# An attention and top-k kernel on one core: where the query split, the selection's flags and the one-hot steps stand in the lists of POOL and DVE

## The chip, the cores and the metric

One of the eight cores of a Trainium2 chip runs the whole program. The metric is the device time of one execution in microseconds, and lower is better. The kernel before took 926.11 us (median of three runs, 923.66 to 931.63). The engines are named as the profile names them: PE multiplies matrices (PEld is its weight load), DVE is the vector engine, ACT the scalar engine, POOL is GpSimd, SP issues most of the DMAs.

## The reference

```python
# attention; q is (4, 12288, 128), kv is (4, 384, 32, 128)
kv_pool = kv.reshape(B, H // 4, 4, W // 4, 4, C).mean(axis=(2, 4))
k = v = kv_pool.reshape(B, -1, C) @ w_sr          # 768 keys a batch
s = (q @ k.transpose(0, 2, 1)) / np.sqrt(C)
a = np.exp(s - s.max(-1, keepdims=True))
x = (a / (a.sum(-1, keepdims=True) + 1e-09)) @ v
# routed MLP: per batch, the 128 tokens with the largest score
scores = np.einsum('bsd,d->bs', x, w_gate)
top_idx = np.argpartition(-scores[b], capacity)[:capacity]
h = np.maximum(x[b, top_idx] @ w1, 0.0)
g = 1.0 / (1.0 + np.exp(-scores[b, top_idx]))
out[b, top_idx] = x[b, top_idx] + g[:, None] * (h @ w2)
```

## The kernel before

The queries are cut into blocks of 256 rows, 48 blocks a batch and 192 in all. The main loop makes one pass over `i` for each block. In pass `i` DVE takes the row maxima of block `i` (`s_max`, the tile `m`), PE makes the scores of block `i + 1` (`S`), ACT makes the exponentials of block `i` (`exp`, the tile `am`), and PE multiplies the probabilities of block `i - 4` by the values (`AV`, into the PSUM tile `o_two`; `LAG` is 4). The probabilities go through `hl`: ACT writes the high halves (`to_high`), POOL the low halves of 1280 columns (`to_low(i, 0, pool)`), DVE those of 256 columns, and two DMA transposes, issued by SP, bring them to `at`. After that DVE normalizes block `i - 4`: `sums`, `recip` (which adds two halves of `o_two` into its columns 260 to 388) and `finish`, the last reader of `o_two`, which writes `x`. The order on each engine is the order in which the program is written: `InOrder` ties each instruction to the one before it on its engine.

Three kinds of further work are generators, which the loop moves on by one step at named places (`at_point`, lines 765 to 812). A generator says with `yield "d"` that its next step belongs at the place "d", which is the last of a pass.

- `next_keys(b + 1)` (line 344) runs during batch `b`, so in the first three batches. For each of six key tiles it has six steps at "d", in which POOL adds up the 16 taps: four quarter sums, one sum over the whole tile, and two last sums, which write `pooled`. One pass after the "d" that follows, at "pe", `key_tile` (line 406) multiplies `pooled` by the weights on PE (two matmuls in the trace's names `s<-pooled,w_k` and `s<-w_in,pooled`). "pe" lies on PE between the high and the low half of `AV`. For the keys of batch 1 the generator starts at once, so that `pooled` is written in passes 5, 11, 17, 23, 29 and 35, all odd, and multiplied two passes later. For batches 2 and 3 it first lets five passes go by, and `pooled` falls in even passes.
- `topk(b)` (line 558) selects the 128 largest scores of batch `b` during the following batch (the last batch is done after the loop in another way). It turns the scores into an integer `key`, finds the threshold of the upper 16 bits in 16 steps of one pass each, makes flags (`gth`, `eqh`, `rest`), finds the threshold of the lower bits in 16 more steps, and makes `mask`. Key, flags and masks stand at "d", each once a batch.
- `pick(b, mask)` (line 604) turns the masks into indices by one-hot matrices (`ge`, then `oh`), gathers the rows, runs the MLP on them and writes them back.

`split_q` (line 422) cuts a pair of query blocks into a high part (`qh`, ACT) and a low part (`ql`, POOL), for `S`. In even passes `i` it is called on line 771 for blocks `i + 2` and `i + 3`, ahead of the pass's `to_low(i, 0, pool)` and behind the "d" of pass `i - 1`. The first use of `ql` is the second matmul of `S(i + 2)`, in pass `i + 1`.

Of the kernel before, what the change touches and what calls it, by code (L numbers as in the profile page):

```python
# [9 lines left out]
BF16 = mybir.dt.bfloat16  # L10
I32 = mybir.dt.int32
U32 = mybir.dt.uint32
U16 = mybir.dt.uint16
AF = mybir.ActivationFunctionType
ALU = mybir.AluOpType
# [4 lines left out]
P = 128  # L20
# [12 lines left out]
VC = C + 2  # L33
# [37 lines left out]
def attention_topk_mlp(ctx, tc, a, outs, capacity):  # L71
# [350 lines left out]
    def split_q(b, blk):  # L422
        ch, h = divmod(blk, BPC)
        raw = qraw[b, ch][:, h * BLK:(h + 2) * BLK]
        qh = qs.tile([P, 2 * BLK], F32R, name="qh")
        ql = qs.tile([P, 2 * BLK], BF16, name="ql")
        act.copy(qh, raw)
        pool.tensor_tensor(out=ql, in0=raw, in1=qh.bitcast(F32), op=ALU.subtract)
        for i in range(2):
            h, l = (x[:, i * BLK:(i + 1) * BLK] for x in (qh, ql))  # L430
            qsplit[b, blk + i] = h, h.bitcast(BF16).rearrange("p (q s) -> p q s", s=2)[:, :, 1], l
# [75 lines left out]
    def turn(n, h):  # L507
        k = cut(n) if by_pe(n) else 2 * M
        sp.dma_start_transpose(out=st[n]["at"][:, h, 0:k // P], in_=st[n]["hl"][:, h, 0:k])
# [26 lines left out]
    def recip(n):  # L536
        b, blk = blocks[n]
        dve.reciprocal(st[n]["rz"], st[n]["rz"])
        if st[n]["two"]:
            st[n]["o"] = o_two[:, :, 2 * VC:2 * VC + VL]  # L540
            dve.tensor_reduce(out=st[n]["o"], in_=o_two[:, :, 0:2 * VC].rearrange("p j (h c) -> p j c h", h=2)[:, :, 0:VL], axis=AX.X, op=ALU.add)
        if b not in scores:
            scores[b] = tk.tile([P, NCOL], F32, name="sc")
        dve.tensor_tensor(out=scores[b][:, blk * QT:(blk + 1) * QT], in0=st[n]["o"][:, :, C], in1=st[n]["rz"], op=ALU.mult)
# [13 lines left out]
    def topk(b):  # L558
        sc = scores.pop(b)
        th = tk.tile([P, 1], F32, name="th")  # L560
        pool.memset(th, float(1 << 15))
        tl = tk.tile([P, 1], F32, name="tl")
        pool.memset(tl, float(1 << 15))
        yield "d"
        key = tk.tile([P, NCOL], I32, name="key")
        dve.tensor_scalar(out=key, in0=sc.bitcast(I32), scalar1=31, scalar2=-(1 << 31), op0=ALU.arith_shift_right, op1=ALU.bitwise_or)
        dve.tensor_tensor(out=key, in0=key, in1=sc.bitcast(I32), op=ALU.bitwise_xor)
        halves = key.bitcast(U16).rearrange("p (n h) -> p n h", h=2)
        low, high = halves[:, :, 0], halves[:, :, 1]
        junk, eqh, rest, gth = (tk.tile([P, NCOL], t, name=x) for x, t in (("junk", BF16), ("eqh", U16), ("rest", U16), ("gth", BF16)))  # L570

        def search(x, t, need):
            for s in range(15, -1, -1):
                yield "cmp"
                cnt = tk.tile([P, 1], BF16, name="cnt")
                dve.tensor_scalar(out=junk, in0=x, scalar1=t, scalar2=None, op0=ALU.is_ge, op1=ALU.add, accum_out=cnt)
                yield "pe"
                pe.matmul(room["count"], ones16, cnt, start=True, stop=True)
                yield "up"
                up = tk.tile([P, 1], F32, name="up")  # L580
                dve.tensor_scalar(out=up, in0=room["count"], scalar1=need, scalar2=float(1 << s), op0=ALU.is_ge, op1=ALU.mult)
                yield "t"
                dve.tensor_scalar(out=t, in0=up, scalar1=-float(1 << (s - 1)) if s else -1.0, scalar2=t, op0=ALU.add, op1=ALU.add)

        yield from search(high, th, float(capacity))
        yield "d"
        above, need = tk.tile([P, 1], BF16, name="cnt"), tk.tile([P, 1], F32, name="need")
        dve.tensor_scalar(out=gth, in0=high, scalar1=th, scalar2=None, op0=ALU.is_gt, op1=ALU.add, accum_out=above)
        dve.tensor_scalar(out=eqh, in0=high, scalar1=th, scalar2=None, op0=ALU.is_equal)
        dve.tensor_tensor(out=rest, in0=low, in1=eqh, op=ALU.mult)  # L590
        yield "pe"
        pe.matmul(room["count"], ones16, above, start=True, stop=True)
        yield "up"
        dve.tensor_scalar(out=need, in0=room["count"], scalar1=-1.0, scalar2=float(capacity), op0=ALU.mult, op1=ALU.add)
        yield from search(rest, tl, need)
        yield "d"
        mask = tk.tile([P, 2, NCOL], BF16, name="mask")
        dve.scalar_tensor_tensor(out=mask[:, 0], in0=rest, scalar=tl, in1=gth, op0=ALU.is_gt, op1=ALU.add)
        dve.scalar_tensor_tensor(out=mask[:, 1], in0=rest, scalar=tl, in1=eqh, op0=ALU.is_equal, op1=ALU.mult)
        yield from pick(b, mask)  # L600
# [3 lines left out]
    def pick(b, mask):  # L604
# [20 lines left out]
        copy(ecol[0:NCOL], e_ps[0:NCOL])  # L625
        yield "d"
        dve.tensor_tensor(out=ecx[0:NCOL], in0=ecol[0:NCOL], in1=inc[0:NCOL, :, P - 1], op=ALU.subtract)
        yield "d"
        copy(pay[0:NCOL, :, 0], ecx[0:NCOL])
        for j0 in range(0, capacity, P):  # L630
            n = min(P, capacity - j0)
# [7 lines left out]
                dve.tensor_scalar(out=jr, in0=small, scalar1=float(j0), scalar2=None, op0=ALU.add)  # L639
            took = tk.tile([P, 2], F32, name="took")  # L640
            for s in range(2):
                dve.tensor_scalar(out=ge[0:NCOL, s], in0=jr[0:NCOL], scalar1=ecol[0:NCOL, s:s + 1], scalar2=None, op0=ALU.is_ge, op1=ALU.add, accum_out=took[0:NCOL, s:s + 1])
            yield "d"
            for s in range(2):
                dve.scalar_tensor_tensor(out=oh[0:NCOL, s], in0=jr[0:NCOL], scalar=ecx[0:NCOL, s:s + 1], in1=ge[0:NCOL, s], op0=ALU.is_ge, op1=ALU.subtract)
            yield "pe"
            g_ps = small_psum([P, P])
# [91 lines left out]
    def at_point(point):  # L739
        advance(vals, point)  # L740
        for tasks in (select, prep) if point == "pe" else (prep, select):
            advance(tasks, point)
# [4 lines left out]
    for i in range(nb):  # L747
        old = i >= LAG
        b, blk = blocks[i]
        if blk % 2 == 0 and i + AHEAD < nb and i + AHEAD >= BPC:  # L750
            nb_, nblk = blocks[i + AHEAD]
            load_q(nb_, nblk // BPC, nblk % BPC * BLK, (nblk % BPC + 2) * BLK)
        if blk == 0 and b + 1 < B:
            start(prep, next_keys(b + 1))
        if i == 0:
            sp.dma_start(out=w1, in_=a["w1"])
            sp.dma_start(out=w2, in_=a["w2"].rearrange("(t f) d -> f t d", f=P))
            ahead.append(load_kv(1, 2))
        if i:
            borrow(s_flat[(i - 1) % 2])  # L760
        s_max(i)
        if old:
            for j in range(QT):
                AV(i - LAG, j, halves=(0,))
            at_point("pe")
            for j in range(QT):
                AV(i - LAG, j, halves=(1,))
        else:
            at_point("pe")
        if i % 2 == 0 and i + 2 < nb:  # L770
            split_q(*blocks[i + 2])
        InOrder.seen.clear()
        at_point("ev")
        bank1 = list(InOrder.seen)
        InOrder.seen.clear()
        at_point("up")
        at_point("g")
        more = 0 < i < nb - 1
        bank0 = list(InOrder.seen)
        if more:  # L780
            if not old:
                warm(12, s_flat[(i + 1) % 2][:, 1024:1024 + P], bank0 + bank1)
            free = {3: bank0 + bank1, 2: bank0, 1: bank0, 0: ()}
            for part, term in ((3, LOW), (2, LOW), (3, HIGH), (2, HIGH)):
                S(i + 1, part, term, free[part])
        exp(i, 2 if by_pe(i) else 1)
        if by_pe(i):
            turn_pe(i)
        exp(i, 1 if by_pe(i) else 2)
        InOrder.seen.clear()  # L790
        at_point("a")
        for x in InOrder.seen:
            for y in st[i + 1]["far"]:
                tc.declare_no_dep(x, y, reason="other banks")
        if more:
            for part, term in ((1, HIGH), (0, HIGH), (1, LOW), (0, LOW)):
                S(i + 1, part, term, free[part])
        to_high(i, 1)
        if old:
            sums(i - LAG)  # L800
            recip(i - LAG)
            finish(i - LAG)
        at_point("t")
        at_point("cmp")
        at_point("v")
        to_low(i, 1, dve)
        exp(i, 0)
        to_high(i, 0)
        turn(i, 0)
        to_low(i, 0, pool)  # L810
        turn(i, 1)
        at_point("d")
        if old and blocks[i - LAG][1] == NBLK - 1:
            start(select, topk(blocks[i - LAG][0]))
# [272 lines left out]
```

## Time and profile before

| | us |
|---|---|
| median of three runs | 926.11 |
| lowest and highest | 923.66, 931.63 |
| the profiled execution | 927.06 |
| its span, first to last instruction | 925.3 |
| PE busy | 874.1 |
| DVE busy | 791.3 |
| POOL busy | 747.3 |
| ACT busy | 741.8 |

A pass is told in the trace by the start of DVE's reduction `m<-s`: there are 192, and the distance of two is the time of a pass. A line of the timeline gives start and duration in us, the engine, the operation, the tiles it writes and reads, and in brackets the engine's idle time before it with what ended it. Transfers and weight loads that lie close together are merged into one line with a count.

### The profile page before, as it was taken

The page shows a single profiled execution, that of the slowest core. Times are in us where ns is not written, and L with a number is a line of the kernel's source. Part 1 is how long each engine was busy: PE and PEld are TensorE (multiplying, and loading weights), DVE is VectorE, ACT ScalarE, POOL GpSimd, SP SyncE. Part 2 cuts the span into 40 slices and gives each one's busy share as a digit, 9 for nine tenths or more (in the row PEclk, how much of TensorE's full clock was granted, in tenths as well). Part 3 has the DMA queues.
Part 4 walks back from the last instruction along what each step waited for, and adds up shares of the span by engine and source line. Part 5 has one row for each costly group of instructions (what it writes and reads, how often), then busy time and mean ns, then how long its engine had stood idle before and what let it go on. Part 6 is the DMA issues. An engine that isn't in the chain of part 4 may idle for free.

```text
span 925.3 us, 21379 instructions
## 1 busy us (share of the span) xinstructions
PE 874.1 (94%) x7785; PEld 683.6 (74%) x7785; DVE 791.3 (86%) x1935; ACT 741.8 (80%) x1148; POOL 747.3 (81%) x486
## 2 busy tenths in 40 slices
PE   4899999999999999999999999999999999999966
PEld 3578778777777767777787777777787777777756
DVE  5888888888898888898889889898879999999943
ACT  2788888889878777888978888788898999888831
POOL 2699999989788888988888989888888877777732
PEclk9999999999999999999999999999999999999999
DMA  8999999999999999999999999999999999999990
GB/s 312 302 210 235 253 235 244 217 219 213 216 221 208 238 227 247 237 232 230 211 216 232 244 213 224 243 247 238 212 222 215 247 243 234 251 247 247 236 181 27
DMA packets 564124, 211.10 MB, mean 228 GB/s; under 512 B 532368, under 2 KB 533648, under 8 KB 563376
## 3 DMA queue, kind: packets, MB, share of 16 engines
q1 hardware_dynamic: 563696, 209.06, 109.4%
q8 instruction: 61, 1.00, 0.5%
q0 software_dynamic: 320, 0.66, 0.3%
q14 instruction: 47, 0.39, 0.1%
HBM read 52.04 MB, written 25.49 MB: 84 GB/s over the span
## 4 chain that ended last, share of the span: by engine, by line
PE 51%; DVE 16%; POOL 11%; DMA 9%; issue 7%; ACT 4%; DVEq 0%; POOLq 0%; SPq 0%; another core or an unknown queue 0%; ACTq 0%
PE s L56 28%; PE o_two L56 23%; DMA at<-hl 8%; DVE m L56 6%; POOL hl L56 5%; POOL kv_sum L56 3%; ACT am L56 2%; POOL ql L56 2%; DVE o_two L56 2%; DVE hl L56 1%; DVE rz L56 1%; DVE x L56 1%; DMA kv_raw<-in_kv 1%; ACT hl L56 1%; DVE kv_raw L56 1%
## 5 line engine op out<-in xcount | busy, mean ns | idle before, releaser
L56 POOL TENSOR_TENSOR hl<-am,hl 128x1280 bf16<-128x1280 f32 x192 | 504.1, 2626 | 125.0 <-ACT hl L56 88.9
L56 PEld LDWEIGHTS <-at 128*128 128x128 f16 (+1 forms) x4656 | 363.9, 97 | 95.3 <-DMA at<-hl 17.9
L56 PE MATMUL o_two<-vx,at 128*128 128x259 f16 (+1 forms) x4548 | 421.8, 246 | 11.8 <-DMA at<-hl 8.4
L56 ACT ACTIVATE am<-s,m 128x512 f32<-128x512 f32 (+1 forms) x528 | 357.9, 706 | 51.1 <-DVE m L56 36.2
L56 DVE TENSOR_REDUCE m<-s 128x2 f32<-128x1536 f32 x192 | 336.4, 1752 | 14.1 <-PE s L56 13.0
L56 ACT CAST hl<-am 128x1280 f16<-128x1280 f32 x192 | 241.6, 1258 | 6.0
L56 PE MATMUL s<-kb,ql 128*128 128x512 bf16 (+1 forms) x769 | 240.2, 326 | 3.2 <-POOL ql L56 3.2
L56 PE MATMUL s<-kl,qh 128*128 128x512 bf16 (+1 forms) x769 | 241.8, 328 | 0.4 <-ACT ecol L56 0.4
L56 PE MATMUL s<-kh,qh 128*128 128x512 f32 (+1 forms) x769 | 215.7, 376 | 1.2 <-ACT kh L56 0.7
L56 DVE TENSOR_REDUCE o_two<-o_two 128x258 f32<-128x516 f32 x188 | 128.4, 683 | 0.0
L56 POOL TENSOR_TENSOR ql<-q_raw,qh 128x512 bf16<-128x512 f32 x96 | 122.4, 1275 | 2.0 <-ACT qh L56 2.0
L56 PEld LDWEIGHTS s<-kh,qh 128*128 128x128 f32 x769 | 116.5, 190 | 6.2 <-ACT kh L56 0.9
L56 PEld LDWEIGHTS <-qh 128*128 128x128 bf16 x769 | 74.8, 97 | 52.9 <-issue 29.6
L56 ACT CAST at<-s 128x256 f16<-128x256 f32 x144 | 53.6, 372 | 67.1 <-PE s L56 67.1
L56 PEld LDWEIGHTS <-ql 128*128 128x128 bf16 x769 | 75.4, 98 | 33.7 <-POOL ql L56 7.9
L56 DVE TENSOR_SCALAR rz<-o_two,sg 128x2 f32<-128x2 f32 x189 | 41.2, 218 | 44.0 <-PE o_two L56 41.3
L56 DVE TENSOR_TENSOR x<-o_two,rz 128x256 f32<-128x256 f32 x189 | 78.4, 415 | 0.0
L56 DVE TENSOR_TENSOR at<-s,at 128x256 bf16<-128x256 f32 x144 | 60.8, 422 | 9.7 <-ACT at L56 4.7
L56 PE MATMUL s<-cst,am 128*128 128x128 f32 x288 | 56.1, 276 | 4.4 <-ACT am L56 4.0
L56 ACT CAST qh<-q_raw 128x512 fp32r<-128x512 f32 x96 | 58.8, 613 | 0.0
L56 POOL TENSOR_TENSOR kv_sum<-kv_raw 128x256 f32<-128x256 f32 x72 | 52.4, 728 | 0.0
L56 PEld LDWEIGHTS s<-cst,am 128*128 128x128 f32 x288 | 35.7, 139 | 16.8 <-ACT am L56 11.0
(163 smaller groups left out, 528.9 us busy)
## 6 DMA issues: line engine op xcount, KB each, us to landing
out<-x SPq DMA_DIRECT2D x96, 256.0 KB, 3.3
q_raw<-in_q SPq DMA_DIRECT2D x94, 256.0 KB, 3.3
kv_raw<-in_kv SPq DMA_DIRECT2D x37, 512.0 KB, 4.9
at<-hl SPq DMA_TRANSPOSE x384, 3.9
kv_raw<-in_kv SPq DMA_DIRECT2D x5, 1024.0 KB, 8.5
w<-in_w SPq DMA_DIRECT2D x2, 512.0 KB, 10.7
kv_raw<-in_kv SPq DMA_DIRECT2D x2, 256.0 KB, 4.8
q_raw<-in_q SPq DMA_DIRECT2D x1, 512.0 KB
```

The costliest lines, as they stand in the source:

```text
L56: r = f(*args, **kwargs)
```

## The change

`split_q` for blocks `i + 3` and `i + 4` is called at the end of odd passes `i`, behind `to_low(i, 0, pool)` and ahead of that pass's "d"; before, the same blocks were split at the start of the even pass behind it. (Pass 0 still splits blocks 2 and 3.) Key, flags and masks move from "d" to a new place "k", which lies between `recip` and `finish`; the place "t" (the threshold's update) moves ahead of `finish` as well. `gth` and `eqh` move from SBUF to columns of `o_two` in PSUM that the attention leaves free, and the first half of the key is written there too. The four one-hot instructions, which stood two and two at two "d" places, stand one each at "cmp", "d", "cmp" and "d" of the same two passes.

```diff
--- before.py
+++ after.py
@@ -562,12 +562,16 @@
         tl = tk.tile([P, 1], F32, name="tl")
         pool.memset(tl, float(1 << 15))
         yield "d"
+        yield "k"
+        side = [o_two[:, j, 2 * VC + VL:2 * VC + VL + NCOL] for j in range(2)]
+        flip = side[0].bitcast(I32)
         key = tk.tile([P, NCOL], I32, name="key")
-        dve.tensor_scalar(out=key, in0=sc.bitcast(I32), scalar1=31, scalar2=-(1 << 31), op0=ALU.arith_shift_right, op1=ALU.bitwise_or)
-        dve.tensor_tensor(out=key, in0=key, in1=sc.bitcast(I32), op=ALU.bitwise_xor)
+        dve.tensor_scalar(out=flip, in0=sc.bitcast(I32), scalar1=31, scalar2=-(1 << 31), op0=ALU.arith_shift_right, op1=ALU.bitwise_or)
+        dve.tensor_tensor(out=key, in0=flip, in1=sc.bitcast(I32), op=ALU.bitwise_xor)
         halves = key.bitcast(U16).rearrange("p (n h) -> p n h", h=2)
         low, high = halves[:, :, 0], halves[:, :, 1]
-        junk, eqh, rest, gth = (tk.tile([P, NCOL], t, name=x) for x, t in (("junk", BF16), ("eqh", U16), ("rest", U16), ("gth", BF16)))
+        junk, rest = (tk.tile([P, NCOL], t, name=x) for x, t in (("junk", BF16), ("rest", U16)))
+        gth, eqh = side
 
         def search(x, t, need):
             for s in range(15, -1, -1):
@@ -583,17 +587,17 @@
                 dve.tensor_scalar(out=t, in0=up, scalar1=-float(1 << (s - 1)) if s else -1.0, scalar2=t, op0=ALU.add, op1=ALU.add)
 
         yield from search(high, th, float(capacity))
-        yield "d"
+        yield "k"
         above, need = tk.tile([P, 1], BF16, name="cnt"), tk.tile([P, 1], F32, name="need")
         dve.tensor_scalar(out=gth, in0=high, scalar1=th, scalar2=None, op0=ALU.is_gt, op1=ALU.add, accum_out=above)
         dve.tensor_scalar(out=eqh, in0=high, scalar1=th, scalar2=None, op0=ALU.is_equal)
-        dve.tensor_tensor(out=rest, in0=low, in1=eqh, op=ALU.mult)
+        dve.tensor_tensor(out=rest, in0=eqh, in1=low, op=ALU.mult)
         yield "pe"
         pe.matmul(room["count"], ones16, above, start=True, stop=True)
         yield "up"
         dve.tensor_scalar(out=need, in0=room["count"], scalar1=-1.0, scalar2=float(capacity), op0=ALU.mult, op1=ALU.add)
         yield from search(rest, tl, need)
-        yield "d"
+        yield "k"
         mask = tk.tile([P, 2, NCOL], BF16, name="mask")
         dve.scalar_tensor_tensor(out=mask[:, 0], in0=rest, scalar=tl, in1=gth, op0=ALU.is_gt, op1=ALU.add)
         dve.scalar_tensor_tensor(out=mask[:, 1], in0=rest, scalar=tl, in1=eqh, op0=ALU.is_equal, op1=ALU.mult)
@@ -625,7 +629,7 @@
         copy(ecol[0:NCOL], e_ps[0:NCOL])
         yield "d"
         dve.tensor_tensor(out=ecx[0:NCOL], in0=ecol[0:NCOL], in1=inc[0:NCOL, :, P - 1], op=ALU.subtract)
-        yield "d"
+        yield "cmp"
         copy(pay[0:NCOL, :, 0], ecx[0:NCOL])
         for j0 in range(0, capacity, P):
             n = min(P, capacity - j0)
@@ -639,9 +643,13 @@
                 dve.tensor_scalar(out=jr, in0=small, scalar1=float(j0), scalar2=None, op0=ALU.add)
             took = tk.tile([P, 2], F32, name="took")
             for s in range(2):
+                if s and not last:
+                    yield "d"
                 dve.tensor_scalar(out=ge[0:NCOL, s], in0=jr[0:NCOL], scalar1=ecol[0:NCOL, s:s + 1], scalar2=None, op0=ALU.is_ge, op1=ALU.add, accum_out=took[0:NCOL, s:s + 1])
-            yield "d"
+            yield "d" if last else "cmp"
             for s in range(2):
+                if s and not last:
+                    yield "d"
                 dve.scalar_tensor_tensor(out=oh[0:NCOL, s], in0=jr[0:NCOL], scalar=ecx[0:NCOL, s:s + 1], in1=ge[0:NCOL, s], op0=ALU.is_ge, op1=ALU.subtract)
             yield "pe"
             g_ps = small_psum([P, P])
@@ -767,8 +775,8 @@
                 AV(i - LAG, j, halves=(1,))
         else:
             at_point("pe")
-        if i % 2 == 0 and i + 2 < nb:
-            split_q(*blocks[i + 2])
+        if i == 0:
+            split_q(*blocks[2])
         InOrder.seen.clear()
         at_point("ev")
         bank1 = list(InOrder.seen)
@@ -799,8 +807,11 @@
         if old:
             sums(i - LAG)
             recip(i - LAG)
+            at_point("t")
+            at_point("k")
             finish(i - LAG)
-        at_point("t")
+        else:
+            at_point("t")
         at_point("cmp")
         at_point("v")
         to_low(i, 1, dve)
@@ -809,6 +820,8 @@
         turn(i, 0)
         to_low(i, 0, pool)
         turn(i, 1)
+        if i % 2 and i + 3 < nb:
+            split_q(*blocks[i + 3])
         at_point("d")
         if old and blocks[i - LAG][1] == NBLK - 1:
             start(select, topk(blocks[i - LAG][0]))
```

## Rows read from the trace of the kernel before

**Rows 1.** Starts of DVE's row maxima (tile m): durations, first to last start.

```profile
L56 DVE TENSOR_REDUCE m<-s x5: 1757/1758/1758, 60.6 to 77.6; 128x2 f32<-128x1536 f32 x5
...
L56 DVE TENSOR_REDUCE m<-s x5: 1746/1748/1749, 519.1 to 536.2; 128x2 f32<-128x1536 f32 x5
...
L56 DVE TENSOR_REDUCE m<-s x13: 1746/1747/1748, 716.5 to 765.3; 128x2 f32<-128x1536 f32 x13
```

**Rows 2.** The waits: who waited for whom, us in total, times, longest.

```profile
PEld L56 <- POOL ql L56: 7.9, 15, 1.1
...
PEld s L56 <- POOL pooled L56: 3.3, 11, 0.4
```

**Rows 3.** One pass of batch 1 in which PE waits for ql, by tile m.

```profile
L56 DVE TENSOR_REDUCE m<-s x2: 1747/1752/1758, 283.1 to 287.7; 128x2 f32<-128x1536 f32 x2
```

**Rows 4.** Timeline of batch 0: POOL, and the weight loads around the key projection.

```profile
107.52 1.43 PEld L56 LDWEIGHTS <-at 128*128 128x128 f16 x12
...
108.47 0.42 POOL L56 TENSOR_TENSOR pooled<-kv_sum 128x128 f32<-128x128 f32 x1
108.84 1.27 POOL L56 TENSOR_TENSOR ql<-q_raw,qh 128x512 bf16<-128x512 f32 x1
108.96 0.30 PEld L56 LDWEIGHTS s<-pooled,w_k 128*128 128x128 f32 x2
...
110.08 2.62 POOL L56 TENSOR_TENSOR hl<-am,hl 128x1280 bf16<-128x1280 f32 x1
```

**Rows 5.** Timeline of batch 1: the same engines, with selection running beside them.

```profile
284.16 1.27 POOL L56 TENSOR_TENSOR ql<-q_raw,qh 128x512 bf16<-128x512 f32 x1
...
285.48 0.10 PEld L56 LDWEIGHTS <-ql 128*128 128x128 bf16 x1 [0.52 <-POOL ql L56]
...
288.68 0.41 POOL L56 TENSOR_TENSOR pooled<-kv_sum 128x128 f32<-128x128 f32 x1
289.14 0.30 PEld L56 LDWEIGHTS s<-pooled,w_k 128*128 128x128 f32 x2 [0.28 <-POOL pooled L56]
```

**Rows 6.** Timeline of pass 3: the first pair that the loop splits.

```profile
38.02 0.72 POOL L56 TENSOR_TENSOR kv_sum<-kv_raw 128x256 f32<-128x256 f32 x1
...
40.02 0.10 PEld L56 LDWEIGHTS <-ql 128*128 128x128 bf16 x1 [1.09 <-POOL ql L56]
```

**Rows 7.** Tiles key and oh: duration in ns, minimum/median/maximum; first and last start.

```profile
L56 DVE TENSOR_TENSOR key<-key,sc x3: 1246/1248/1249, 256.0 to 703.5; 128x96 int32<-128x96 int32 x3
...
L56 DVE TENSOR_TENSOR rest<-key,eqh x3: 258/259/701, 337.9 to 773.8; 128x96 uint16<-128x96 uint16 x3
...
L56 DVE SCALAR_TENSOR_TENSOR oh<-jrow,ecx,ge x6: 336/454/1421, 435.2 to 864.8; 96x128 bf16<-96x128 bf16 x6
```

**Rows 8.** Tile m over two passes, those with the key, then those with the masks.

```profile
L56 DVE TENSOR_REDUCE m<-s x3: 1745/1757/1757, 251.7 to 261.3; 128x2 f32<-128x1536 f32 x3
...
L56 DVE TENSOR_REDUCE m<-s x3: 1744/1748/1758, 699.1 to 708.4; 128x2 f32<-128x1536 f32 x3
...
L56 DVE TENSOR_REDUCE m<-s x3: 1745/1748/1757, 412.3 to 421.3; 128x2 f32<-128x1536 f32 x3
...
L56 DVE TENSOR_REDUCE m<-s x3: 1746/1748/1749, 841.3 to 850.9; 128x2 f32<-128x1536 f32 x3
```

**Rows 9.** Timeline: finish (x) and the next block's AV, in batches 0, 3 and 3.

```profile
72.26 0.42 DVE L56 TENSOR_TENSOR x<-o_two,rz 128x256 f32<-128x256 f32 x1
...
73.17 1.06 PE L56 MATMUL o_two<-vx,at 128*128 128x259 f16 x8
...
747.90 0.41 DVE L56 TENSOR_TENSOR x<-o_two,rz 128x256 f32<-128x256 f32 x1
...
748.59 0.61 PE L56 MATMUL o_two<-vx,at 128*128 128x259 f16 x4
...
707.45 0.41 DVE L56 TENSOR_TENSOR x<-o_two,rz 128x256 f32<-128x256 f32 x1
...
707.91 0.27 PE L56 MATMUL o_two<-vx,at 128*128 128x259 f16 x1 [0.76 <-DVE x L56]
```

## The prediction

> **What bounds the kernel now.** I read the page's busy times first: of a span of 925.3 us PE is busy 874.1, which is 94%, and DVE, POOL and ACT 80 to 86%. So a microsecond won on another engine is won in time only where PE stands still for it. Next the passes, by the starts of the row maxima [rows 1]. A quiet pass takes 17.0 / 4 = 4.25 us in batch 0, 17.1 / 4 = 4.28 us in batches 1 and 2 with selection beside it, and 48.8 / 12 = 4.07 us in batch 3, where no keys are prepared. These are the floors; what the change can win or lose shows as passes above them. Last the waits [rows 2] and, for each edit, the timeline of a pass that holds it.
>
> **The query split, batches 1 and 2.** PE's weight loads wait 15 times for `ql`, 7.9 us of idle weight loading in all [rows 2]. One such wait: `ql` ends at 285.43 and the load of it comes at 285.48 [rows 5]. The pass in which that falls takes 4.6 us, from 283.1 to 287.7 [rows 3], against 4.28; told to the hundredth it is 0.35 us more. There are eleven such passes, 3.9 us together. With the split ahead of the "d" sums, `ql` comes before the whole-tile sum of 1.27 us, and this wait is gone.
>
> But the pass after each of these holds a key projection, and there the weights' load waits for `pooled`: it ends at 289.09, the load comes at 289.14 [rows 5]. Between `ql` and `pooled` POOL has no idle time: one `hl` of about 2.6 us, one sum of about 0.6 us, then `pooled`. The change puts `ql` before the first of these sums and leaves the same work between the same two points, so `pooled` ends when it did. What PE gains in front of the projection it loses at it. I take 0 for all eleven; the other end is the whole 3.9 us.
>
> **The query split, batch 0.** Here the parity is the other one. `pooled` is written in odd passes, and there the order before was `hl`, sum, `pooled`, `ql`, `hl`. `pooled` ends at 108.47 + 0.42 = 108.89, and PE's load for the projection comes at 108.96 [rows 4]. PE had weight loads of `at` until 107.52 + 1.43 = 108.95. So `pooled` is just in time and there is no slack. After the change `ql` goes ahead of the two last sums. It holds POOL from 108.84 to the start of the next `hl` at 110.08, so 1.24 us. `pooled` then ends at 110.13 and the load comes at 110.20 instead of 108.96. Behind that load on PE, which runs in program order, stand the low half of `AV` and all of `S(i + 1)`; the row maxima and the exponentials wait for these. PE has no idle time in these passes to make it up with (4.25 us is its floor), so the pass gets longer by 1.24 us. Batch 0 has six key tiles, all in odd passes: 6 x 1.24 = +7.4 us. The bounds are 0 and 7.4.
>
> **The first pair.** In pass 3 `ql` waits behind a sum of 0.72 us and PE's load waits 1.09 us for it [rows 6]. The swap takes the 0.72 us off. DVE still has two constants to copy in that pass, so not all of it is won: -0.4 us, between 0 and -0.7.
>
> SP has no new work by the swap. The ACT half, `qh`, keeps its place behind `to_high`; both only change sides with "d".
>
> **Key, flags, masks.** Two passes with a key take 9.6 us [rows 8] against 8.55 of the floor, so 1.05 above it (batch 2 the same), and in batch 3 9.3 against 8.13, so 1.2. The key's second instruction takes 1246 ns, while `rest`, of the same kind and width, takes 258 when nothing is in its way [rows 7]. It waited for POOL's `ql` to end. With one operand in PSUM I take 0.3 us for it, the nearest row being 258; the other end is the 1246 of before. At "k" the two key instructions cost about 0.6 us, and they now delay `finish`. The next block's `AV` overwrites `o_two` and must wait for that. In batches 0 to 2 `x` ends at 72.68 and `AV` starts at 73.17; in batch 3 it is 748.31 and 748.59; and where `AV` does wait, it starts 0.05 us after `x` (707.86 and 707.91) [rows 9]. So the room is 0.44 us, and in batch 3 0.23. What is left of the delay is 0.16 and 0.37 us. Gain: 2 x (1.05 - 0.16) + (1.2 - 0.37) = 2.6 us.
>
> The masks, two instructions, by the same working: 9.0 against 8.55, 0.45 above, twice; in batch 3 9.6 against 8.13, 1.45, of which I give about 0.3 to a wait for a transpose in that stretch. 2 x (0.45 - 0.16) + (1.15 - 0.37) = 1.4 us. Of the flags only one `rest` was held up (701 against 258 ns [rows 7]), and in its new place the group of about 0.8 us costs 0.3 to 0.5 us at `AV` each time; I take 0, from -0.5 to +0.5. The threshold's update, 0.2 us ahead of `finish` in 96 passes, fits the room of 0.44 and just fits 0.23: 0, at most +0.6.
>
> The Trainium skill (SBUF — State Buffer, Who interferes with whom) says that a DVE instruction with two SBUF inputs and a GpSimd instruction that reads SBUF exclude each other for the whole instruction, and that the one that starts first wins. The rows agree for the key. By that rule the new key, flags and masks are free of POOL, while `oh`, which keeps two SBUF inputs, is not; the sum would be the same by it for key and masks, and higher by up to 3 us for `oh`.
>
> **One-hot steps.** `ge` was never stretched; a first `ge` at "cmp" fills an idle stretch of DVE: -0.2 us in batch 3, 0 in the others, where POOL sets the passes. `oh` takes 336 to 1421 ns [rows 7]. At its old place it stood behind DVE's 0.42 us of low halves and met only the tail of POOL's `ql` in batches 1 and 2. At "cmp" it comes about 0.65 us sooner, into the body of that `ql`, and everything behind it on DVE, the low halves and the next row maxima, waits. I take +0.4 us in each of two batches and 0 in the third: +0.6 us with `ge`. The ends are -1.2 and +3.
>
> **Sum.** +7.4 - 0.4 - 2.6 - 1.4 + 0.6 = +3.6 us. The profiled execution took 927.06 us (span 925.3), 0.95 above the median; its changed time would be 930.7, and on the median of 926.11 that is 929.7. I predict 929.7 us. The likeliest case alone runs from 926 to 933, by the bounds of key, masks and one-hot steps and the 8 us over which the three runs before spread.
>
> **Rivals.**
>
> A, not slower: the sums in batch 0 cost nothing, because the projection has room that the trace hides. It decides at `pooled` ending by 108.95; 0.06 us of room is all that the timeline shows, against a delay of 1.24 [rows 4]. Then 926.11 - 3.8 = 922.3. Chance 0.12.
>
> B: the waits for `ql` in batches 1 and 2 are won for good, since PE is earlier and POOL's chain shortens with it. For it speaks that its waits are the larger row, 7.9 against 3.3 us [rows 2]; against it that POOL is without a gap from `ql` to `pooled`. Then 929.7 - 3.9 = 925.8. Chance 0.11. A and B together give 918.4, chance 0.06.
>
> C, slower still: `oh` at "cmp" waits for a whole POOL instruction of 1.3 to 2.6 us each time, or the longer passes of batch 0 push transposes into waits of their own. Three times 1.0 to 1.3 more, and some 1 to 2 us of transposes: 934 to 936. Chance 0.10.
>
> D: the edit doesn't do what it says, and the PSUM operand doesn't free the key and masks from POOL. Then the 4.0 us of both are not won: 933.7. Chance 0.05.
>
> The Trainium skill's rule of exclusion (same page and section) bears on C and D: it speaks against D, and for the `oh` part of C.
>
> **The numbers.** My forecast has 0.56. The range 921.5 to 934.5 takes in A, B, D and the likeliest case's own range, and leaves out A with B together and most of C. A measurement of this kernel can tell about 1% from no change, so 916.8 and 935.4 are the limits. Faster by over 1% needs A and B and more: 0.06. Slower by over 1% needs C or its parts on top of the forecast: 0.10. Within 1%: 0.84.
>
> **What would show it.** In batch 0, six passes longer by 1.24 us than they were, with PE's projection waiting for `pooled`, which stands behind `ql` on POOL. In batches 1 and 2 no waits for `ql`, and waits for `pooled` longer by about 0.35 us. The key's second instruction at about 300 ns, two passes with a key at about 8.7 us, and `AV` after it waiting for `x`. `oh` still stretched, as often as not by `ql`. The prediction is wrong if those six passes keep their length, or if those of batches 1 and 2 fall by 0.35 without the projection's wait growing.

## The result, and the profile after

The changed kernel takes 931.43 us (median of seven runs, 929.38 to 934.24), and the kernel before 926.37 on the same chips (seven runs, 922.37 to 931.63). The ratio is 1.0064, with an interval from 1.0039 to 1.0089: +3.6 to +8.2 us, +5.9 by the ratio itself and +5.1 by the two medians. The forecast was +3.6 us and 929.7, in a range from 921.5 to 934.5.

The profiled execution took 929.38 us. The page of the kernel after, its span and the engines' busy times:

```profile
span 927.6 us, 21262 instructions
PE 863.9 (93%) x7665; PEld 682.2 (74%) x7785; DVE 784.4 (85%) x1935; ACT 742.3 (80%) x1148; POOL 747.4 (81%) x486
```

No engine is busy for more than 0.5 us longer than before. (120 matmul records are missing, so PE's busy time can't be compared.) What changed is what PE waits for. The waits of the kernel after, by engine, tile and releaser: us in total, times, longest.

```profile
PEld L56 <- DMA at<-hl: 17.9, 20, 2.0
PEld s L56 <- POOL pooled L56: 13.1, 15, 1.2
PE o_two L56 <- DVE x L56: 4.3, 7, 1.6
PEld L56 <- POOL ql L56: 0.8, 2, 0.4
```

Beside [rows 2]: the wait for `ql` has gone from 7.9 to 0.8 us, as the edit means it to, and the wait for `pooled` has come up from 3.3 to 13.1. The transposes (`at<-hl`) cost the same 17.9 us in both.

In batch 0 no weight load waited for `pooled` before; now all six projections do, 1.21 to 1.23 us each and 7.4 us together. The other 5.7 us lie in batches 1 and 2, which had the 3.3 before. Timeline of the kernel after in batch 0, of POOL and the projection's weight load, the pass that answers to [rows 4]:

```profile
111.23 1.28 POOL L56 TENSOR_TENSOR ql<-q_raw,qh 128x512 bf16<-128x512 f32 x1
...
112.47 0.62 POOL L56 TENSOR_TENSOR kv_sum<-kv_sum 128x256 f32<-128x256 f32 x1
...
113.16 0.41 POOL L56 TENSOR_TENSOR pooled<-kv_sum 128x128 f32<-128x128 f32 x1
113.53 2.62 POOL L56 TENSOR_TENSOR hl<-am,hl 128x1280 bf16<-128x1280 f32 x1
113.63 0.30 PEld L56 LDWEIGHTS s<-pooled,w_k 128*128 128x128 f32 x2 [1.23 <-POOL pooled L56]
```

`ql` now holds POOL from 111.23 to the sum at 112.47, 1.24 us; `pooled` comes after it, and PE's load has waited 1.23 us. The passes tell the price. Tile `m` (count, durations in ns, first and last start) over the 32 passes that hold batch 0's six projections, before and then after:

```profile
L56 DVE TENSOR_REDUCE m<-s x33: 1757/1758/1758, 51.6 to 190.7; 128x2 f32<-128x1536 f32 x33
```

```profile
L56 DVE TENSOR_REDUCE m<-s x33: 1756/1758/1758, 52.7 to 199.0; 128x2 f32<-128x1536 f32 x33
```

139.1 us against 146.3: 7.2 more, in six passes of 5.91 us that were 4.71. That is more than the whole difference of the medians. Selection gave something back. Tile `key` of the kernel after:

```profile
L56 DVE TENSOR_TENSOR key<-o_two,sc x3: 256/257/258, 267.3 to 713.6; 128x96 int32<-128x96 int32 x3
L56 DVE TENSOR_SCALAR_CACHE_REDUCE o_two<-key,th x3: 320/322/322, 343.4 to 778.8; 128x96 f32<-128x96 uint16 x3
L56 DVE DVE_READ_ACCUMULATOR o_two<-key,th x3: 143/143/144, 343.7 to 779.1; 128x1 bf16 x3
L56 DVE TENSOR_SCALAR o_two<-key,th x3: 320/321/321, 343.9 to 779.3; 128x96 f32<-128x96 uint16 x3
L56 DVE TENSOR_TENSOR rest<-o_two,key x3: 257/257/257, 344.2 to 779.6; 128x96 uint16<-128x96 f32 x3
```

The key's second instruction, 1248 ns in [rows 7], takes 257, and `rest` is never held up. Tile `oh`, which keeps two operands in SBUF, went the other way: its median was 454 ns and is now 763.

```profile
L56 DVE SCALAR_TENSOR_TENSOR oh<-jrow,ecx,ge x6: 333/763/1027, 440.2 to 868.0; 96x128 bf16<-96x128 bf16 x6
```

### The profile page after: what moved, and what is told of

Its sections match the earlier page's. It is cut to its first block, busy times and chain, and to the rows that moved or that the text cites. A ratio compares the mean times of both kernels' runs of the same rounds, so it can differ in the third digit from the quotient of the medians.

```text
span 927.6 us, 21262 instructions
## 1 busy us (share of the span) xinstructions
PE 863.9 (93%) x7665; PEld 682.2 (74%) x7785; DVE 784.4 (85%) x1935; ACT 742.3 (80%) x1148; POOL 747.4 (81%) x486
## 4 chain that ended last, share of the span: by engine, by line
PE 49%; DVE 12%; POOL 11%; DMA 10%; ACT 10%; issue 7%; SPq 0%; POOLq 0%; DVEq 0%; another core or an unknown queue 0%; ACTq 0%
PE s L56 26%; PE o_two L56 23%; DMA at<-hl 8%; DVE m L56 6%; ACT am L56 5%; POOL hl L56 5%; POOL kv_sum L56 3%; ACT hl L56 3%; POOL ql L56 2%; DMA kv_raw<-in_kv 2%; ACT s L56 2%; DVE hl L56 1%; DVE o_two L56 1%; DVE junk L56 1%; DVE rz L56 1%
## 5 line engine op out<-in xcount | busy, mean ns | idle before, releaser
L56 PEld LDWEIGHTS <-at 128*128 128x128 f16 (+1 forms) x4656 | 362.3, 97 | 97.6 <-DMA at<-hl 17.9
L56 PE MATMUL s<-kb,ql 128*128 128x256 bf16 (+1 forms) x740 | 230.6, 324 | 5.1 <-issue 0.2
L56 PE MATMUL s<-kl,qh 128*128 128x512 bf16 (+1 forms) x678 | 209.8, 322 | 1.0
```

The lines of the kernel that those rows point to most:

```text
L56: r = f(*args, **kwargs)
```

## The experiments

The ratios below are against the kernel before on the same chip, where nothing else is said: 35 runs with a median of 927.5 us for the first four kernels, 32 runs with 928.8 for the others, except two kernels that have one run each. A ratio is estimated from these runs together with its interval, so it is not quite the quotient of the two medians. Two kinds of number are read: the ratio, whose interval is 0.5 to 0.7% wide, and, in one profiled execution of each kernel, the time of the one to three passes that hold an edit, which is the same to 0.02 us in every kernel that has the edit in the same place and no transpose to wait for.

**The split back at its old place, and the split alone.** First the changed kernel with only `split_q` put back:

```diff
-        if i == 0:
-            split_q(*blocks[2])
+        if i % 2 == 0 and i + 2 < nb:
+            split_q(*blocks[i + 2])
...
-        if i % 2 and i + 3 < nb:
-            split_q(*blocks[i + 3])
         at_point("d")
```

> The changed kernel with the query split back at its old place (start of the even pass, behind the sums of the odd one); key, flags, masks and one-hot steps stay as changed. My theory: the split alone costs 7.2 us (six passes of batch 0, 1.2 us each) and wins nothing in batches 1 and 2, so this kernel is about 1.3 us below the kernel before (key -2.6, masks -0.2, flags +0.7, one-hot +0.8 by the passes of the changed trace), ratio about 0.9985, and the six passes are back at 4.71 us. Rival (the waits for ql in batches 1 and 2 are a real gain of 3.9 us): the split's cost is then only 3.3 us, and this kernel is about 1.8 us above the kernel before.

928.44 us, ratio 1.0004 (0.998 to 1.0029), which takes in what the theory and what the rival expects; the passes decide below. The other way round, the kernel before with the same lines changed the opposite way and nothing else:

> The kernel before with nothing but the query split moved. My theory: six passes of batch 0 at 5.9 us, +7.2 us, nothing won in batches 1 and 2, at most 0.4 us in pass 3: ratio about 1.0075. Rival (ql waits are a real gain): +3 us, ratio about 1.003.

933.97 us, ratio 1.0063 (1.0038 to 1.0087). So the split by itself costs as much as the whole change, as far as the totals can tell. Its six passes in batch 0 are 5.90 us, as in the changed kernel, and 4.71 with the split back. Rival A, that the projection has room, has fallen.

The same two runs decide batches 1 and 2. Timeline of the kernel with the split put back, in batch 2:

```profile
514.34 0.10 PEld L56 LDWEIGHTS <-ql 128*128 128x128 bf16 x1 [0.54 <-POOL ql L56]
...
517.51 0.42 POOL L56 TENSOR_TENSOR pooled<-kv_sum 128x128 f32<-128x128 f32 x1
517.99 0.30 PEld L56 LDWEIGHTS s<-pooled,w_k 128*128 128x128 f32 x2 [0.27 <-POOL pooled L56]
```

And of the changed kernel, the same two passes, which start at 514.52:

```profile
516.37 0.10 PEld L56 LDWEIGHTS <-ql 128*128 128x128 bf16 x1
...
520.13 0.42 POOL L56 TENSOR_TENSOR pooled<-kv_sum 128x128 f32<-128x128 f32 x1
...
520.60 0.30 PEld L56 LDWEIGHTS s<-pooled,w_k 128*128 128x128 f32 x2 [0.66 <-POOL pooled L56]
```

The wait of 0.54 us for `ql` is gone, and that for `pooled` has grown from 0.27 to 0.66. Tile `m` over the pair, in the kernel before and in the kernel after:

```profile
L56 DVE TENSOR_REDUCE m<-s x3: 1747/1749/1758, 509.3 to 519.1; 128x2 f32<-128x1536 f32 x3
```

```profile
L56 DVE TENSOR_REDUCE m<-s x3: 1758/1758/1758, 514.5 to 524.3; 128x2 f32<-128x1536 f32 x3
```

9.8 us both times (9.75 and 9.76 told to the hundredth, 9.75 with the split put back): 4.64 + 5.12 has become 4.29 + 5.47. Of ten such pairs (the two that hold the one-hot steps are left out), seven differ by 0.1 us or less between these two kernels. The other three are shorter by 0.11 to 0.58, and with the split put back as well, so it isn't the split that makes them so. Rival B has fallen too.

**The early split from batch 1 on.**

```diff
-        if i == 0:
-            split_q(*blocks[2])
+        if i % 2 == 0 and i + 2 < nb and blocks[max(i - 1, 0)][0] == 0:
+            split_q(*blocks[i + 2])
...
-        if i % 2 and i + 3 < nb:
+        if i % 2 and i + 3 < nb and b:
             split_q(*blocks[i + 3])
```

> The changed kernel with the split at its old place in batch 0 and at its new place from batch 1 on. My theory: no stall in batch 0 and no gain in batches 1 and 2, so the same time as the kernel with the split wholly undone, about 1.3 us below the kernel before, at most 1.3 us better where a pass has room. In batches 1 and 2 a pass with the old ql wait falls by 0.35 us and the next one, with the projection, grows by as much. Rival: 3.9 us below the kernel with the split undone, 5 us below the kernel before (0.9945).

927.68 us, ratio 0.9998 (0.9976 to 1.0021). Batch 0 is back at 4.72 us a projection, and the total is that of the kernel with the split put back; the rival's 0.9945 lies outside the interval. So in batches 1 and 2 the early split neither costs nor gives anything that the total shows, and all that it costs lies in batch 0. (The passes show one gain: the pair with the one-hot steps takes 10.79 and 10.78 us here and 11.07 with the split put back.)

**The one-hot steps back, two and two, at "d".**

```diff
-        yield "cmp"
+        yield "d"
         copy(pay[0:NCOL, :, 0], ecx[0:NCOL])
...
-                if s and not last:
-                    yield "d"
...
-            yield "d" if last else "cmp"
+            yield "d"
...
-                if s and not last:
-                    yield "d"
```

> The changed kernel with the four one-hot instructions back at their old places, two and two at d. My theory: oh at cmp runs into POOL's ql, which costs 0.45 us in each of batches 1 and 2 and nothing in batch 3, so this kernel is 0.8 us below the changed one, about 4.2 us above the kernel before; the pair of passes 89 and 90 takes 10.34 us instead of 10.79. Rival (spreading them helps, since DVE is never held for 0.9 us at a stretch): this kernel is slower than the changed one by 0.5 us or more.

933.48 us, ratio 1.0071 (1.0047 to 1.0094): the totals can't tell it from the changed kernel. The pairs can. With the old one-hot steps the two passes take 10.13 and 10.12 us in batches 1 and 2, with the spread ones 10.80 and 10.78; in batch 3 it is 9.84 against 9.72. Spreading costs 0.67 and 0.66 us and wins 0.11 once. The expected 10.34 was the pair of the kernel before; the early split takes 0.2 off that, since the kernel with the split alone has 10.13 and 10.10. The cause is in the timeline of the changed kernel:

```profile
439.78 1.30 POOL L56 TENSOR_TENSOR ql<-q_raw,qh 128x512 bf16<-128x512 f32 x1
...
440.20 1.02 DVE L56 SCALAR_TENSOR_TENSOR oh<-jrow,ecx,ge 96x128 bf16<-96x128 bf16 x1
```

`oh` starts at 440.20, inside POOL's `ql`, and ends 0.14 us after it; in the same pass, free of it, the other `oh` takes 0.33 us. With the old one-hot steps this `oh` takes 0.36, which is the 0.67 us.

**The key alone, with its first half in PSUM and then in SBUF.** The kernel before with this change only, and beside it the same with `flip` an SBUF tile:

```diff
+        yield "k"
+        flip = o_two[:, 0, 2 * VC + VL:2 * VC + VL + NCOL].bitcast(I32)
         key = tk.tile([P, NCOL], I32, name="key")
-        dve.tensor_scalar(out=key, in0=sc.bitcast(I32), ...)
-        dve.tensor_tensor(out=key, in0=key, in1=sc.bitcast(I32), op=ALU.bitwise_xor)
+        dve.tensor_scalar(out=flip, in0=sc.bitcast(I32), ...)
+        dve.tensor_tensor(out=key, in0=flip, in1=sc.bitcast(I32), op=ALU.bitwise_xor)
...
+            at_point("k")
             finish(i - LAG)
```

> The kernel before with one part of the change alone: the key at the new place, its first half in PSUM. My theory: three passes taken together, 13.93, 13.88 and 13.40 us, fall to 12.98, 12.97 and 12.63, 2.6 us in all, ratio about 0.997. Rival (what the row maxima win is lost where AV waits for finish): no change.

925.28 us, ratio 0.9975 (0.9943 to 1.0007). The three passes from the key on take 13.00, 12.99 and 12.75 us; they were 13.93, 13.88 and 13.40. That is 2.5 us by the passes; the total alone can't tell it from no change.

> The kernel before with the key at its new place, but with its first half in SBUF as it was, so that the second key instruction has two inputs in SBUF. It tells the place from the PSUM column. My theory (an instruction with two SBUF inputs waits for the POOL instruction that runs): in batches 1 and 2 the key stands under POOL's hl, so the second instruction takes up to 0.9 us instead of 0.26, and three passes with it take 13.5 to 13.7 us instead of 12.98; in batch 3 likewise. Rival (the place alone won it): 13.0 us, the second instruction about 260 ns.

One run each: 927.41 us beside 924.7. The three passes take 13.74, 13.68 and 13.55, so of the gain 0.19 and 0.20 us are left in batches 1 and 2, and batch 3 loses 0.15. That is near what was expected. But it was not the expected instruction that waited. Timeline of this kernel, and then of the changed one:

```profile
257.64 2.62 POOL L56 TENSOR_TENSOR hl<-am,hl 128x1280 bf16<-128x1280 f32 x1 [0.34 <-POOL ql L56]
...
259.22 1.11 DVE L56 TENSOR_SCALAR flip<-sc 128x96 int32<-128x96 int32 x1
260.36 0.26 DVE L56 TENSOR_TENSOR key<-flip,sc 128x96 int32<-128x96 int32 x1
```

```profile
265.31 2.63 POOL L56 TENSOR_TENSOR hl<-am,hl 128x1280 bf16<-128x1280 f32 x1 [0.34 <-POOL tl L56]
...
267.00 0.26 DVE L56 TENSOR_SCALAR o_two<-sc 128x96 int32<-128x96 int32 x1
267.30 0.26 DVE L56 TENSOR_TENSOR key<-o_two,sc 128x96 int32<-128x96 int32 x1
```

`flip<-sc` reads one SBUF tile, writes another, and does not end before POOL's `hl` has ended at 260.26; the second instruction then meets no POOL work. With its output in PSUM the first takes 0.26 us under an `hl` of the same length. The Trainium skill (SBUF — State Buffer, Who interferes with whom) lists `tensor_scalar` among the DVE operations that can enter a mode that takes the pair of ports shared with GpSimd, for the whole instruction. The 1.11 us here agree with it.

**The flags in SBUF, at the new place.** The changed kernel with

```diff
-        junk, rest = (tk.tile([P, NCOL], t, name=x) for x, t in (("junk", BF16), ("rest", U16)))
-        gth, eqh = side
+        junk, eqh, rest, gth = (tk.tile([P, NCOL], t, name=x) for x, t in (("junk", BF16), ("eqh", U16), ("rest", U16), ("gth", BF16)))
```

> The changed kernel with gth and eqh in SBUF and in 16-bit types as before, at the new place. In the changed kernel the flag group of batch 3 costs 0.57 us more a pair than before (8.97 against 8.40). My theory: this is the place (finish, and with it AV, stands behind the group); in SBUF the group is 0.15 us shorter in its three first instructions, but rest and the two masks have two SBUF inputs and wait for POOL's hl, up to 0.6 us each where one runs, so the pairs with flags and masks take as long or longer. Rival (writing the flags to PSUM is what costs): the pair of batch 3 falls back to 8.4 us.

One run each: 930.79 us beside 924.7 of the kernel before. Each pair of passes with the masks takes 10.47 to 10.52 us instead of 8.92 to 9.44. Timeline of this kernel:

```profile
415.62 2.64 POOL L56 TENSOR_TENSOR hl<-am,hl 128x1280 bf16<-128x1280 f32 x1 [0.97 <-ACT hl L56]
417.52 0.86 DVE L56 SCALAR_TENSOR_TENSOR mask<-rest,tl,gth 128x96 bf16<-128x96 uint16 x1
418.22 1.28 POOL L56 TENSOR_TENSOR ql<-q_raw,qh 128x512 bf16<-128x512 f32 x1
418.30 1.32 DVE L56 SCALAR_TENSOR_TENSOR mask<-rest,tl,eqh 128x96 bf16<-128x96 uint16 x1
...
420.00 1.50 PE L56 MATMUL o_two<-vx,at 128*128 128x259 f16 x12 [1.65 <-DVE x L56]
```

The first mask waits for the end of `hl`, the second for the end of `ql`, and `AV` 1.65 us for `x` behind them. With the flags in PSUM both masks together take 0.54 us. So at "k" the PSUM columns are needed. The flags' own pair in batch 3 can't be compared by its time: 9.23 us with SBUF has a wait of 0.75 us for a transpose in it, against 8.97 with PSUM and 8.40 before. The waits of `AV` for `x` can: none before, 0.62 us with the flags in SBUF at the new place, 0.80 with them in PSUM. So most of it is the place, and PSUM adds about 0.2.

**Where the projection's waiting should go.** If the parity of `pooled` against `ql` is what decides, it can be set the other way. First the changed kernel with batch 1's keys begun one pass later, so that `pooled` falls in the passes in which POOL has no `ql`:

```diff
-        lead, wait = (2, 0) if b == 1 else (1, 5)
+        lead, wait = (2, 1) if b == 1 else (1, 5)
```

> The changed kernel, with the keys of batch 1 begun one pass later, so that pooled falls in even passes in batch 0 too and the moved ql no longer stands directly ahead of it. My theory: the projection's pass loses 1.24 us of its stall and gets the smaller wait of batches 1 and 2 (0.64 us a pair): the six pairs of batch 0 go from 10.17 to about 9.75 us, 0.4 to 0.55 us each, so 2.5 to 3.3 us below the changed kernel, about 2 us above the kernel before (1.002). Rival (the stall comes from the split being sooner as such, in whatever pass the sums end): no change from the changed kernel.

933.63 us, ratio 1.0054 (1.0023 to 1.0085): a miss. A projection's two passes went from 10.17 to 9.79 us, six times, so 2.3 us were won, as expected. But ACT's copies of the keys now stand in the passes in which it also copies the queries. Timeline of this kernel, ACT:

```profile
97.29 0.62 ACT L56 CAST qh<-q_raw 128x512 fp32r<-128x512 f32 x1
97.81 0.40 ACT L56 CAST kh<-kv_proj 128x256 fp32r<-128x256 f32 x1
98.12 0.40 ACT L56 CAST kb<-kv_proj 128x256 bf16<-128x256 f32 x1
98.43 1.04 ACT L56 ACTIVATE am<-s,m 128x512 f32<-128x512 f32 x2
```

The three passes of batch 0 that hold them grew from 4.26 to 4.73 (4.75 once). That leaves 0.9 us of the 2.3, too little for these intervals to show.

Then the kernel before, with the keys of batches 2 and 3 begun one pass sooner, which puts `pooled` in batches 1 and 2 on the side that batch 0 has:

```diff
-        lead, wait = (2, 0) if b == 1 else (1, 5)
+        lead, wait = (2, 0) if b == 1 else (1, 4)
```

> The kernel before, with one number changed: for the keys of batches 2 and 3 the generator lets four passes go by instead of five, so that pooled falls in odd passes there too, ahead of ql, as in batch 0. My theory (whether ql stands between the last two hl ahead of a projection decides): neither the wait for ql nor the wait for pooled is left in batches 1 and 2; a pass ahead of a projection takes 4.29 us, the one with it 4.83, so a pair 9.12 instead of 9.75 to 10.08, eleven times 0.64 = 7.0 us, ratio about 0.9925. Rival (POOL as a whole has too much to do in these batches, in whatever order): the waits stay and the time is that of the kernel before.

922.4 us (ten runs, 916.98 to 925.88), ratio 0.9918 (0.9886 to 0.9949). The waits of this kernel:

```profile
PEld L56 <- DMA at<-hl: 22.1, 27, 2.2
...
PEld L56 <- POOL ql L56: 2.1, 3, 1.1
```

There is no row for `pooled` any more, and the one for `ql` has gone from 7.9 to 2.1, of which 1.9 are those of batch 0. The pair at 9.75 us takes 9.12 (tile `m` of this kernel over that pair):

```profile
L56 DVE TENSOR_REDUCE m<-s x3: 1748/1750/1750, 508.4 to 517.6; 128x2 f32<-128x1536 f32 x3
```

So in these kernels the order within POOL's list only moves the wait from `ql` to `pooled`, and the phase of the key sums against the query splits takes both away.

**Both.** The key's edit and the earlier keys on the kernel before:

> The two above that should win, together, on the kernel before: the key at its new place and four passes of waiting instead of five. My theory: the gains lie in different passes and add up, 7.0 + 2.6 = 9.6 us, ratio about 0.9896. Rival (a faster stretch makes the transposes late and PE waits for at instead): the waits for at grow and less than half of it, under 4.8 us, is left.

921.75 us (eleven runs, 913.96 to 923.6), ratio 0.9906 (0.9874 to 0.9939). It is faster than the kernel before, by 0.6 to 1.3%. PE's waits for `at` came to 19.8 us, so the rival did not come. That the key's edit adds to the earlier keys is seen in its three passes alone (13.00, 12.99 and 12.75 us); the totals of this kernel and of the one with the earlier keys can't be told apart.

## Why the prediction held, step by step

The terms, and what the passes of the changed kernel measured against those of the kernel before:

| term | predicted, us | measured, us |
|---|---|---|
| batch 0, six projections | +7.4 | +7.2 (5.91 against 4.71, six times) |
| batches 1 and 2, `ql` against `pooled` | 0 | 0 where undisturbed (9.75 and 9.76) |
| first pair, pass 3 | -0.4 | 0 (5.23 both) |
| last pass of batch 0 with key sums | none | -0.46 |
| key | -2.6 | -2.6 (0.95 + 0.91 + 0.77), over three passes |
| masks | -1.4 | -0.3 (0.08 + 0.07 + 0.11), over two passes |
| flags | 0, -0.5 to +0.5 | +0.57 in batch 3, -0.11 in batch 2, open in batch 1 |
| threshold's update | 0 | 0 (quiet passes 4.29 and 4.07, as before) |
| one-hot steps | +0.6 | +0.8 (0.47 + 0.45 - 0.11) |

The measured terms add up to 7.2 - 0.46 - 2.6 - 0.3 + 0.46 + 0.8 = +5.1 us, and the medians differ by 5.06. That they agree so closely is luck: the interval reaches from 3.6 to 8.2. In batch 3 it matters how many passes are counted: over three, as for the key, the masks there give 0.39 and the flags cost 0.70, which leaves the sum at 5.0. The forecast of +3.6 is 1.5 us below the sum of the passes, and the masks alone make 1.1 of it.

**The split, batch 0** was right in mechanism and size. It rested on one reading: `pooled` at 108.89 and the load at 108.96 [rows 4], with no idle time of PE to absorb a delay. **Batches 1 and 2** were right as well: POOL has no gap between `ql` and `pooled` [rows 5], so a `ql` that comes earlier moves nothing behind it.

**Pass 3** was mis-sized. The 1.09 us wait of [rows 6] shrank to 0.41, but the pass kept its 5.23 us. By the timeline DVE's copies of constants, which the prediction named as a reason to take less than 0.72, were the whole of it: in both kernels the second of them runs up to the next row maxima. **A pass that the prediction didn't see** paid for it: the one from 221.1 us, in which the last key work of batch 0 (the values' split) stood on POOL ahead of `ql`. Tile `m` over that pass, before and after:

```profile
L56 DVE TENSOR_REDUCE m<-s x2: 1757/1757/1757, 221.1 to 226.1; 128x2 f32<-128x1536 f32 x2
```

```profile
L56 DVE TENSOR_REDUCE m<-s x2: 1758/1758/1758, 229.4 to 233.6; 128x2 f32<-128x1536 f32 x2
```

4.97 us became 4.27, and the pass two behind it grew by 0.25. The kernels with the late split have 4.96 to 5.00 there.

**The key** was right to the tenth over three passes. Over the two that the prediction names as a sign it is 8.91 and 8.90 us, not 8.7, and the pass behind them gives 0.25 back (4.07 against 4.32). `AV` waited 0.18 and 0.22 us for `x` in batches 1 and 3, where 0.16 and 0.37 were forecast. Rival D has fallen: under a running `hl` the second instruction takes 257 ns with its operand in PSUM.

**The masks** were mis-sized by a factor of five (of about three, if the third pass of batch 3 is counted). Three steps of the prediction failed. The first is the floor: the two passes were set against 8.55 us, two quiet ones, but the second holds PE's own work on the masks, and with nothing held up it takes 4.38 us, not 4.28. The second is what is left of the delay: 0.25 us instead of 0.16, as the masks now stand on DVE ahead of `finish`, of the low halves and of the next row maxima. Before, the pair of 9.0 us [rows 8] was 4.91 + 4.09: the time lost in the first pass was partly made up in the second. Now it is 4.54 + 4.38, in the kernel after:

```profile
L56 DVE TENSOR_REDUCE m<-s x3: 1745/1758/1758, 418.0 to 426.9; 128x2 f32<-128x1536 f32 x3
```

The third is batch 3, where 0.11 us of the forecast 0.78 came over the pair. The prediction gave 0.3 us of that pair to a wait for a transpose, but PE's weight load waits 1.15 us for `at` in that pass before and 1.19 after, and 1.2 to 2.0 in the other ten kernels. What an edit gives in one pass is to be read from the pair, and the pair's floor from a pair that holds the same matmuls.

The terms of masks and split are not independent, which the prediction did not see either. With the early split and the masks at "d" (the kernel with the split alone) the second mask stands under `ql`:

```profile
424.22 1.33 DVE L56 SCALAR_TENSOR_TENSOR mask<-rest,tl,eqh 128x96 bf16<-128x96 uint16 x1
```

That pair takes 9.54 and 9.55 us in batches 1 and 2, against 9.00 before and 8.92 in the changed kernel. So beside the early split the masks' move is worth 0.62 us a batch; against the kernel before it looks like 0.08.

**The flags** cost what the far bound said. The group takes 1.0 us at "k", and `AV` waits. Timeline of the changed kernel in batch 1:

```profile
343.45 0.32 DVE L56 TENSOR_SCALAR_CACHE_REDUCE o_two<-key,th 128x96 f32<-128x96 uint16 x1
343.68 0.14 DVE L56 DVE_READ_ACCUMULATOR o_two<-key,th 128x1 bf16 x1
343.86 0.32 DVE L56 TENSOR_SCALAR o_two<-key,th 128x96 f32<-128x96 uint16 x1
344.22 0.26 DVE L56 TENSOR_TENSOR rest<-o_two,key 128x96 uint16<-128x96 f32 x1
344.39 0.41 DVE L56 TENSOR_TENSOR x<-o_two,rz 128x256 f32<-128x256 f32 x1
...
344.86 1.39 PE L56 MATMUL o_two<-vx,at 128*128 128x259 f16 x11 [0.57 <-DVE x L56]
```

The 0.57 us are a group of 1.0 against a room of 0.44 [rows 9]. In batch 2 it is made up by `rest` no longer being held up there; in batch 1 the pair holds waits for transposes in every kernel with the change (10.3 to 11.0 us), so its share stays open.

**The one-hot steps** were nearly right against the kernel before (+0.47 and +0.45 us, forecast +0.4). The mechanism was the one forecast, an `oh` in the body of `ql`. The Trainium skill's rule of exclusion (SBUF — State Buffer, Who interferes with whom) bears on this term, and the 1.02 us under `ql` agree with it. That the size fits is in part luck: the run with the old steps shows that the spread costs 0.67 us a batch beside an early split, and 0.2 of it is hidden by what the early split gives in the same pair. With the split put back the spread costs 0.74 (11.07 against 10.33). Rival C in its full form, a whole POOL instruction at each `oh`, didn't come: the longest was 1.03 us.

What the prediction couldn't give is the difference of two single executions: the two profiled ones differ by 2.3 us, the medians by 5.1. The transposes' waits alone came to 13.0 to 30.0 us over the profiled kernels, with no order by edit (17.9 in both main kernels, 30.0 with the split put back, 24.7 with the split alone). One pass of the profiled execution after, the first, took 4.88 us where all others have 3.75; the kernels with the same code there don't show it. What sets these two is open.

## What to carry to other kernels

An instruction moved up a queue delays everything that it passes: find the last of these that another engine waits for, and look at how much room it has, one stage at a time, since the same move can cost 1.2 us a turn in one stage and nothing in the next. A wait whose producer's queue has no gap up to the next product that is waited for is not removed by reordering; it moves there. Here the cure was one pass of phase between the two streams of work, key sums and query splits (0.8%, by the ratio 0.9918), not their order within a pass. And two edits that meet in one pass are not to be priced one by one against the kernel before: the early split made the masks' old place worse and the one-hot steps' old place better.

## What the runs showed of the hardware that was not expected

- A plain `tensor_scalar` of 96 columns with one SBUF operand and an SBUF output is held up by a running POOL instruction just as one with two SBUF operands is: `flip` took 1.07 to 1.16 us against 0.26 with the output in PSUM. The form that also sums is not: `ge`, from SBUF to SBUF too, took 0.33 us in the middle of an `hl` (434.76 to 435.09 in the changed kernel).
- The flags took longer at the new place in PSUM: the comparison that also sums 320 to 322 ns, 302 to 313 in SBUF, the read of its accumulator 143 against 84 to 90, the plain comparison 321 against 264 to 269 where no POOL instruction held it up. The three together make 0.13 us, a good part of the room at `AV`. In PSUM the flags are f32 and in SBUF of 16 bits; no run tells the two causes apart.
- Four DVE instructions held up by POOL (`flip`, two masks, `oh`) ended 0.07 to 0.14 us after the POOL instruction under which they started: `flip` at 260.33 after 260.26, the masks at 418.38 and 419.62 after 418.26 and 419.50, `oh` at 441.22 after 441.08.
